# Filler matmuls made 32 columns wide, a scheduler model with tiling switches, and a lent PSUM bank, in an attention and linear-attention stack

## Chip, cores, metric

One core of one Trainium2 chip. The metric is the device time of one execution in microseconds (us). The experiments ran in three sessions on three chips, each with the kernel before in the same rounds; where sessions are compared, go by the ratio to it.

## The reference, cut to what matters

The input is one sequence of 2048 tokens, 512 wide. Four residual blocks run in turn: A, B, A, B.

```python
x = x + _A_ref(_layernorm(x), wq, wk, wv, wo)     # 32 query heads of 16, one shared key/value head
x = x + _B_ref(_layernorm(x), wqkv, wo)           # 32 heads of linear attention
# ... the same two once more
# A: p = softmax(q k^T / 4); o = p v        B: phi(q) (phi(k)^T v) / (phi(q) sum phi(k))
```

Block A needs 32 x 2048 x 2048 exponentials, twice. In tiles of 128 keys by 512 queries that is 2 x 2048 = 4096 tiles. Each needs a score matmul, an exponential and a value matmul, and the exponentials are the work that decides the time.

## The kernel before

The kernel is written as a list of operations with guessed durations. A small event-driven model of the chip runs at build time, decides the order of instructions on every engine, and the program is emitted in that fixed order. What the chip then does differently from the model changes the times, but not the order.

```python
LAT = {PE: 0.2, AC: 0.22, DV: 0.13, PO: 0.2, SP: 2.0}     # us until another engine sees a result
# ... inside fill(): one "set" of up to three score tiles in PSUM banks 3s, 3s+1, 3s+2
def f(e):
    return self.smm(e, got, 3 * s)              # three matmuls, 32 rows x 128 columns each
o  = add(PE, 0.2 + 0.014 * m, f, ...)                                  # score matmuls of a set
oe = add(AC, tac(m * 512), lambda e: e.activation(PTA[...], bank(3 * s, m * 512), ACTF.Exp, scale=SCALE), ...)
# ... add_pv(): a value matmul, 128 rows x 32 columns, into one of four column groups of bank 7
c = (j % NRG) * (4 // NRG) + j // NRG
return e.matmul(ps[32 * c:32 * c + 32, 7 * 512:8 * 512], lhsT=Vaug[:, kt, :], rhs=src, ...)
# ... dstep()/dpass(): the same work for a tile whose exponential VectorE computes, through bank 6,
#     as a polynomial in eight instructions a pair of tiles
```

A score tile thus goes one of two ways: ScalarE takes three at a time from banks 0 to 2 or 3 to 5, VectorE takes single tiles through bank 6. Projections and transposes ("misc") also go through bank 6, unless `SHARE` lets them use bank 5.

To hold TensorE's clock up, the model adds filler matmuls with zero weights whenever TensorE is idle and a running sum is low. That a TensorE with too little to do is granted less clock is what the kernel's author assumes here; what the runs show of it is the granted clock of 0.998 in the kernel before, against 0.851 when its 1234 fillers use 32 rows each (b_rows32, below).

```python
FILL, FILLW, FILLN = 0.6, 1.7, 512
SHARE = False

def idle(now):
    if not sc.order[PE] or streaming(now) > FILL * FILLW:
        return
    # ... (when bank 7 may be written)
    o = add(PE, 0.03 + FILLN * 0.41e-3, lambda e: e.matmul(bank(7, FILLN), lhsT=zer[:],
            rhs=maskx[:].bitcast(BF16)[:, 0:FILLN], start=not owned, stop=True, skip_group_check=True), ...)
```

The filler adds zeros to bank 7, where the value sums grow, and uses the whole array: 128 rows by 128 columns.

The softmax here doesn't subtract the row's maximum and nothing guards it: scores larger than these inputs give would overflow.

Of the kernel before, what the change touches and what calls it, by code (L numbers as in the profile page):

```python
# [5 lines left out]
BF16 = mybir.dt.bfloat16  # L6
# [9 lines left out]
STATS = {}  # L16
FLEX = 0.0


class Op:  # L20
    __slots__ = ("engs", "fn", "dur", "prio", "deps", "nleft", "succ", "rt", "guard", "acq", "uses", "rel", "cb",
                 "eng", "t0", "vis", "idx", "gidx", "waits", "marked", "val", "vc", "dma", "done", "name")

# [22 lines left out]
class Sched:  # L46


    def __init__(self, nc):
        self.nc = nc  # L50
        self.now = 0.0
        self.engs = [PE, AC, DV, PO, SP]
        self.tfree = {e: 0.0 for e in self.engs}
        self.pend = {e: [] for e in self.engs}
        self.ready = {e: [] for e in self.engs}
        self.order = {e: [] for e in self.engs}
        self.events = []
        self.seq = 0
        self.lastw = {}
        self.readers = {}  # L60
        self.all = []
        self.step = lambda now: False
        self.act_ok = lambda op: True
        self.idle = lambda now: None

    def add(self, engs, dur, fn, reads=(), writes=(), prio=5.0, guard=None, acq=(), uses=(), rel=(), cb=None, deps=(),
            dma=False, name=""):
        o = Op()
        o.engs = engs if isinstance(engs, tuple) else (engs,)
        o.dur = dur if isinstance(dur, dict) else {e: dur for e in o.engs}  # L70
        o.fn, o.prio, o.guard, o.acq, o.uses, o.rel, o.cb, o.dma, o.name = fn, prio, guard, acq, uses, rel, cb, dma, name
        o.rt, o.done, o.succ, o.marked = self.now, False, [], False
        ds = [d for d in deps if d is not None]
        for k in reads:
            w = self.lastw.get(k)
            if w is not None:
                ds.append(w)
        for k in writes:
            w = self.lastw.get(k)
            if w is not None:  # L80
                ds.append(w)
            ds += self.readers.get(k, ())
        for k in reads:
            self.readers.setdefault(k, []).append(o)
        for k in writes:
            self.lastw[k] = o
            self.readers[k] = []
        o.deps = []
        seen = set()
        for d in ds:  # L90
            if id(d) not in seen and d is not o:
                seen.add(id(d))
                o.deps.append(d)
        o.nleft = 0
        for d in o.deps:
            if d.done:
                o.rt = max(o.rt, self._vis(d, o))
            else:
                o.nleft += 1
                d.succ.append(o)  # L100
        if o.nleft == 0:
            self._queue(o)
        return o

    def _vis(self, d, o):
        if d.eng == PE and o.engs[0] == PE:
            return d.t0 + d.dur[PE]
        return d.vis

    def _queue(self, o):  # L110
        self.seq += 1
# [7 lines left out]
    def _try(self, e):  # L119
# [7 lines left out]
        if e == DV:  # L127
            cand = sorted(ready, key=lambda r: (r[0] + (FLEX if len(r[2].engs) > 1 and self.act_ok(r[2]) else 0.0), r[1]))
        for i, (p, s, o) in enumerate(cand):
            if o.done:  # L130
                continue
            if e == AC and len(o.engs) > 1 and not self.act_ok(o):
                continue
# [20 lines left out]
    def _start(self, e, o):  # L154
# [9 lines left out]
        for h in tuple(o.acq) + tuple(o.uses):  # L164
            for sl in h.pool.slots(h.idx, h.kind) if hasattr(h.pool, "slots") else (h.idx,):
                h.pool.hist[sl].append(o)
        end = self.now + o.dur[e]
        o.vis = end + (3.0 if o.dma else LAT[e])
        self.tfree[e] = end
        self.at(end, None)  # L170
        self.at(o.vis, None)
# [142 lines left out]
def bass_interleave_layers__grouped_kv_mqa__linear_attn_block__prompt_kernel(  # L314
# [20 lines left out]
    NRG, NM = P // RG, RG // DH  # L335
    FILL, FILLW, FILLN = 0.6, 1.7, 512
    SHARE = False
    FINE = (0, 3)
# [121 lines left out]
    def layer_norm(t, prio, cb, win=None):  # L460
# [15 lines left out]
        def tr(e):  # L476
# [3 lines left out]
            return i  # L480
        o = add(PE, 0.45, tr, reads=["ident"], deps=[o], uses=[hx], acq=[hb], rel=[hx], prio=prio, name="tr")

# [5 lines left out]
    def proj(h, mms, n, reads, prio, chunk=2, name="proj"):  # L488

        o = None  # L490
        for c in range(0, len(mms), chunk):
# [6 lines left out]
            kw = dict(acq=[h]) if c == 0 else dict(uses=[h], deps=[o])  # L498
            o = add(PE, len(part) * (0.03 + n * 0.36e-3), f, reads=reads, prio=prio, name=name, **kw)
        return o  # L500
# [18 lines left out]
    def v_proj(L, t0, n, prio):  # L519
        h = H_()  # L520

        def f(e):
# [4 lines left out]
            return k  # L527
        o = add(PE, 0.16 * n, f, reads=["wv"] + [("xnT", t) for t in range(t0, t0 + n)], acq=[h], prio=prio, name="vp")

# [18 lines left out]
    def q_tile(L, t, prio):  # L548
        h = H_()
        o = None  # L550
        for c in range(0, NG, 2):
# [6 lines left out]
            kw = dict(acq=[h]) if c == 0 else dict(uses=[h], deps=[o])  # L558
            o = add(PE, 0.55, f, reads=["wq", ("xnT", t)], prio=prio, name="qt", **kw)

# [8 lines left out]
    class Ctl:  # L569
# [75 lines left out]
        def add_pv(self, p, src, hold, dep, last):  # L645
# [9 lines left out]
            def cb(o):  # L655
# [10 lines left out]
                if sum(self.count[u]) == 64:  # L666
                    self.norm(u, o)

            def f(e):
                c = (j % NRG) * (4 // NRG) + j // NRG  # L670
                return e.matmul(ps[32 * c:32 * c + 32, 7 * 512:8 * 512], lhsT=Vaug[:, kt, :], rhs=src, start=opened[0], stop=opened[1],  # L671
                                skip_group_check=True)
            o = add(PE, 0.1, f, reads=[("V", kt)], deps=[dep], uses=[hold], rel=[hold] if last else [], prio=2.0 + 1e-4 * u, guard=guard, cb=cb, name="pv")
            return o

        def norm(self, u, last):
# [13 lines left out]
            def tr(e):  # L690
                for qs in range(4):
                    i = e.transpose(bank(ht.idx, P, qs * P), Eo[:, he.idx, qs * P:(qs + 1) * P], identf[:])
                return i
            o = add(PE, 1.0, tr, reads=["identf"], deps=[oe], acq=[ht, hos] if par == 0 else [ht], uses=[he], rel=[he], prio=1.2, name="trA")
            o = add(DV, 0.168, lambda e: e.reciprocal(rden[:, hr.idx, :].unsqueeze(2), bank(ht.idx).rearrange("p (a c) -> p a c", c=32)[:, :, DH:DH + 1]),
# [60 lines left out]
        def fill(self, s, got, kind):  # L756
# [9 lines left out]
            m = len(got)  # L766

            def f(e):
                return self.smm(e, got, 3 * s)
            o = add(PE, 0.2 + 0.014 * m if RG == 32 else 0.05 + 0.14 * m, f, reads=self.keys(got), deps=prev, uses=[h], prio=0.0, name="sA")  # L770
            hp = Holder(p_pta)
# [18 lines left out]
        def dstep(self):  # L790
# [36 lines left out]
            banks.hist[6] = []  # L827
            o = add(PE, 0.22, lambda e: self.smm(e, [p], 6), reads=self.keys([p]), deps=prev, uses=[h], prio=1.5, name="sD")
            o = add(DV, tdv(512), lambda e: e.tensor_scalar(out=xT[:, hx.idx, i * 512:(i + 1) * 512], in0=bank(6), scalar1=SCALE * LOG2E * 65536.0,  # L829
# [45 lines left out]

    def streaming(now):

        tot = 0.0
        for o in reversed(sc.order[PE]):
            if o.t0 + 1.5 < now - FILLW:  # L880
                break
            st = {"pv": 0.071, "sA": 0.2 if RG == 32 else 0.4, "dummy": 0.2}.get(o.name, 0.85 * o.dur[PE])
            end = o.t0 + o.dur[PE]
            if end > now - FILLW:
                tot += st * min(1.0, (end - (now - FILLW)) / o.dur[PE])
        return tot

    def idle(now):
        if not sc.order[PE] or streaming(now) > FILL * FILLW:
            return  # L890
        u = ctl.acc_owner
        owned = u >= 0 and 0 < sum(ctl.count[u]) < 64
        if not owned and not banks.free[7]:
            return
        if owned and now < sc.tfree[AC] < now + 0.1:
            return
        o = add(PE, 0.03 + FILLN * 0.41e-3, lambda e: e.matmul(bank(7, FILLN), lhsT=zer[:], rhs=maskx[:].bitcast(BF16)[:, 0:FILLN], start=not owned, stop=True, skip_group_check=True),  # L897
                reads=["mask", "zer"], deps=[] if owned else list(banks.hist[7]), prio=9.0, name="dummy")
        banks.hist[7].append(o)
        sc._try(PE)  # L900

# [5 lines left out]
    def epi_tr(L, qb, g, hos, fine):  # L907
# [4 lines left out]
        def tr(e):  # L912
# [3 lines left out]
            return i  # L916
        o = add(PE, 0.45, tr, reads=["ident", ("Osb", g % 2, 0), ("Osb", g % 2, 1)], acq=[h], uses=[hos], rel=[hos], writes=keys, prio=pr, name="otr")

# [57 lines left out]
    def pq_tile(t, pr):  # L976
# [3 lines left out]
        for g in range(NG):  # L980
# [4 lines left out]
            kw = dict(acq=[h]) if g == 0 else dict(uses=[h], deps=[o])  # L985
            o = add(PE, 0.27, f, reads=["wqkv", ("xnT", t)], prio=pr, name="pq", **kw)
        phi(h, o, pqT[:, :, ts], [("pq", g, t) for g in range(NG)], 2.4, tiled=True)

    def kv_block(L, b):
        tl = KVB[b]  # L990
        n, final = len(tl), b == len(KVB) - 1
        for hh in range(2):
            h = H_()
            o = None
            for i, t in enumerate(tl):
# [10 lines left out]
                rd = [t] if i > 0 else tl  # L1006
                o = add(PE, 0.22, f, reads=[(k, tt) for k in ("pk", "vB") for tt in rd], prio=3.4, name="kv", **kw)
            dst = kvacc if b == 0 else kvtmp
# [33 lines left out]
    def b_tile(L, t, nxt):  # L1042
# [4 lines left out]
        def den(e):  # L1047
            for g in range(NG):
                i = e.matmul(bank(hd.idx, P, g * P), lhsT=zb[:, g, :], rhs=pqT[:, g, ts], start=True, stop=True)
            return i  # L1050
        o = add(PE, 0.3, den, reads=[("zb", g) for g in range(NG)] + [("pq", g, t) for g in range(NG)], acq=[win, hd], prio=pr - 0.4, name="den")
        o = add(AC, tac(512), lambda e: e.activation(e_buf[:, he.idx, :], bank(hd.idx), ACTF.Ln, bias=1e-6), deps=[o], uses=[hd], acq=[he], rel=[hd], prio=0.4 + 0.01 * t, name="ln")
# [74 lines left out]
```

## Time and profile before

| | before |
|---|---|
| median time (3 runs) | 1779.86 us (1778.36 to 1780.38) |
| ScalarE (ACT) busy | 1728.1 us, 97% |
| VectorE (DVE) busy | 1554.0 us, 87% |
| tiles on ACT / on DVE | 3618 / 478 |
| fillers | 1234 |
| mean granted clock | 0.998 |

From the page of the kernel before: busy times by engine (PEld is TensorE loading weights), the granted TensorE clock in 40 slices (9 is 90% or more), the chain of waits, and groups of instructions (count, busy us, mean ns, idle us of the engine ahead of them and what ended it).

```profile
PE 1683.0 (95%) x11642; PEld 533.4 (30%) x11642; DVE 1554.0 (87%) x2767; ACT 1728.1 (97%) x1452; POOL 31.3 (2%) x46
...
PEclk9999999999999999999999999999999999999999
...
ACT 62%; PE 19%; DVE 17%; issue 1%; DMA 0%; POOL 0%; SPq 0%
...
L775 ACT ACTIVATE PTA<-ps_all 128x1536 bf16<-128x1536 f32 x1207 | 1644.0, 1569 | 7.7 <-PE ps_all L635 6.3
L635 PE MATMUL ps_all<-QT,Kr 32*128 32x512 bf16 x4096 | 611.3, 385 | 39.8 <-ACT PTA L775 14.8
L671 PE MATMUL ps_all<-PTA,Vaug 128*32 128x512 bf16 x3618 | 520.1, 390 | 8.2 <-DVE Eo L683 7.8
L897 PE MATMUL ps_all<-maskx,zer 128*128 128x512 bf16 x1234 | 401.0, 386 | 0.0
L829 DVE TENSOR_SCALAR xT<-ps_all 128x512 int32<-128x512 f32 x478 | 327.4, 685 | 80.8 <-PE ps_all L635 78.9
```

ACT is the bound: 97% busy, and the exponentials (L775) wait only 6.3 us for TensorE in the whole run. TensorE looks nearly as busy, but 401 us of its time are fillers (L897). DVE has time to spare, and 78.9 us of its idle time is spent waiting for its own score tile (L829 waits for L635).

The waits of the kernel before (us in total, times, longest):

```profile
DVE xT L829 <- PE ps_all L635: 78.9, 129, 1.3
DVE e_buf L940 <- ACT e_buf L939: 45.2, 29, 2.8
DVE v_tok L958 <- PE ps_all L496: 25.3, 19, 3.1
...
DVE x_sb L933 <- PE ps_all L496: 11.1, 12, 2.2
```

The timeline of TensorE alone, kernel before (start us, us, engine, line, form rows*columns, count):

```profile
60.02 0.40 PE L671 MATMUL ps_all<-PTA,Vaug 128*32 128x512 bf16 x3
60.35 0.39 PE L897 MATMUL ps_all<-maskx,zer 128*128 128x512 bf16 x1
60.67 0.39 PE L635 MATMUL ps_all<-QT,Kr 32*128 32x512 bf16 x1
```

Three value matmuls of different column groups start within nanoseconds of each other (0.40 us in all for three of 0.39; over the trace 3 ns apart in the median). The filler, in another tiling, starts 0.33 us later, and the next tiling again 0.32 us later. Over the whole trace a change of tiling is 315 to 323 ns start to start in the median, by the kind of change, and two fillers in a row 226 ns.

### The profile page before, as it was taken

What the parts mean: (1) busy time and instruction counts of PE and PEld (TensorE: products, weight loads), DVE (VectorE), ACT (ScalarE), POOL (GpSimd) and SP (SyncE); (2) the same over time, 40 slices, a digit from 0 to 9 for tenths busy, and PEclk for the clock granted to TensorE, in tenths of its full rate; (3) what the DMA queues carried; (4) which work ended last, traced back from release to release, by engine and by line L of the source; (5) the groups of instructions that cost most, each with busy time, mean ns of one, the idle gap of its engine ahead of it and who ended that gap; (6) DMA issues with size and microseconds to landing.
All of it is one profiled execution on the core that took longest, in us unless ns stands there. A gap on an engine that the chain in (4) does not pass through costs nothing.

```text
span 1777.9 us, 27691 instructions
## 1 busy us (share of the span) xinstructions
PE 1683.0 (95%) x11642; PEld 533.4 (30%) x11642; DVE 1554.0 (87%) x2767; ACT 1728.1 (97%) x1452; POOL 31.3 (2%) x46
## 2 busy tenths in 40 slices
PE   7999999999999999999899999999999999999998
PEld 4222222222232222233442222322222322222334
DVE  7999997999887998878789999879998879978775
ACT  7999999999999999999699999999999999999996
POOL 0000000000000000000000000000000000000000
PEclk9999999999999999999999999999999999999999
DMA  3000000000000000000000000000000000000001
GB/s 120 1 1 1 1 1 1 1 1 1 1 1 1 1 1 1 1 1 1 1 1 1 1 1 1 1 1 1 1 1 1 1 1 1 1 1 1 1 1 48
DMA packets 7724, 9.14 MB, mean 5 GB/s; under 512 B 1456, under 2 KB 7088, under 8 KB 7600
## 3 DMA queue, kind: packets, MB, share of 16 engines
q1 hardware_dynamic: 7600, 7.37, 1.3%
q8 instruction: 91, 1.49, 0.3%
q14 instruction: 33, 0.27, 0.1%
HBM read 5.28 MB, written 2.10 MB: 4 GB/s over the span
## 4 chain that ended last, share of the span: by engine, by line
ACT 62%; PE 19%; DVE 17%; issue 1%; DMA 0%; POOL 0%; SPq 0%
ACT PTA L775 60%; PE ps_all L635 6%; PE ps_all L671 5%; PE ps_all L897 3%; DVE xT L829 3%; DVE PTD L851 3%; PE ps_all L496 2%; ACT e_buf L939 1%; DVE xs L847 1%; DVE xu L846 1%; DVE xs L850 1%; DVE stats L461 1%; PE ps_all L1060 1%; DVE xs L848 1%; DVE xu L849 1%
## 5 line engine op out<-in xcount | busy, mean ns | idle before, releaser
L775 ACT ACTIVATE PTA<-ps_all 128x1536 bf16<-128x1536 f32 x1207 | 1644.0, 1569 | 7.7 <-PE ps_all L635 6.3
L635 PE MATMUL ps_all<-QT,Kr 32*128 32x512 bf16 x4096 | 611.3, 385 | 39.8 <-ACT PTA L775 14.8
L671 PE MATMUL ps_all<-PTA,Vaug 128*32 128x512 bf16 x3618 | 520.1, 390 | 8.2 <-DVE Eo L683 7.8
L897 PE MATMUL ps_all<-maskx,zer 128*128 128x512 bf16 x1234 | 401.0, 386 | 0.0
L829 DVE TENSOR_SCALAR xT<-ps_all 128x512 int32<-128x512 f32 x478 | 327.4, 685 | 80.8 <-PE ps_all L635 78.9
L635 PEld LDWEIGHTS ps_all<-QT,Kr 32*128 32x128 bf16 x4096 | 147.2, 91 | 486.3 <-ACT PTA L775 188.1
L851 DVE SCALAR_TENSOR_TENSOR PTD<-xT,xs 128x1024 uint16<-128x1024 int32 x239 | 290.3, 1215 | 1.8
L671 PEld LDWEIGHTS ps_all<-PTA,Vaug 128*32 128x32 bf16 x3618 | 126.2, 93 | 319.0 <-issue 299.9
L846 DVE TENSOR_SCALAR xu<-xT 128x1024 f16<-128x1024 uint16 x239 | 164.3, 687 | 3.7
L847 DVE TENSOR_TENSOR xs<-xu 128x1024 f16<-128x1024 f16 x239 | 163.5, 684 | 2.9
L850 DVE TENSOR_TENSOR xs<-xs,xu 128x1024 f16<-128x1024 f16 x239 | 163.0, 682 | 2.4
L897 PEld LDWEIGHTS ps_all<-maskx,zer 128*128 128x128 bf16 x1234 | 93.9, 97 | 196.5 <-issue 179.4
L671 PE MATMUL ps_all<-PTD,Vaug 128*32 128x512 bf16 x478 | 128.8, 388 | 18.2 <-DVE Eo L683 11.4
L848 DVE TENSOR_SCALAR xs<-xs 128x1024 f16<-128x1024 f16 x239 | 98.9, 414 | 1.7
L849 DVE TENSOR_SCALAR xu<-xu 128x1024 f16<-128x1024 f16 x239 | 99.2, 415 | 0.0
L496 PE MATMUL ps_all<-wqkv_sb,xnT 128*128 128x512 bf16 x256 | 68.7, 382 | 1.5 <-DVE xT L829 0.9
L940 DVE TENSOR_SCALAR e_buf<-e_buf 128x512 f32<-128x512 f32 x64 | 27.1, 423 | 45.4 <-ACT e_buf L939 45.2
L469 POOL TENSOR_TENSOR rstd<-veps,mhalf 128x1 f32<-128x1 f32 x30 | 27.8, 925 | 1668.5 <-DVE veps L467 1668.5
L939 ACT ACTIVATE e_buf<-ps_all 128x512 f32<-128x512 f32 x64 | 46.0, 719 | 4.8 <-PE ps_all L496 3.1
L671 PEld LDWEIGHTS ps_all<-PTD,Vaug 128*32 128x32 bf16 x478 | 28.2, 93 | 65.2 <-DVE PTD L851 30.7
L461 DVE BATCH_NORM_STATS2 stats<-x_sb 128x6 f32<-128x512 bf16 x64 | 43.2, 680 | 3.8 <-DMA x_sb<-in_A_x_dram 2.9
L683 DVE COPY Eo<-ps_all 128x512 f32<-128x512 f32 x62 | 42.4, 684 | 4.3 <-PE ps_all L671 3.7
(87 smaller groups left out, 825.9 us busy)
## 6 DMA issues: line engine op xcount, KB each, us to landing
out_dram<-x_sb SPq DMA_DIRECT2D x16, 128.0 KB, 1.7
x_sb<-in_A_x_dram SPq DMA_DIRECT2D x3, 512.0 KB, 6.9
wqkv_sb<-in_B_wqkv_dram SPq DMA_DIRECT2D x1, 1536.0 KB, 11.3
x_sb<-in_A_x_dram SPq DMA_DIRECT2D x2, 256.0 KB, 3.1
wq_sb<-in_A_wq_dram SPq DMA_DIRECT2D x1, 512.0 KB, 5.1
wo_sb<-in_A_wo_dram SPq DMA_DIRECT2D x1, 512.0 KB, 8.3
wo_sb<-in_B_wo_dram SPq DMA_DIRECT2D x1, 512.0 KB, 10.9
wk_sb<-in_A_wk_dram SPq DMA_DIRECT2D x1, 16.0 KB, 2.5
```

The lines of the kernel that those rows point to most:

```text
L496: i = e.matmul(bank(h.idx, n), lhsT=l, rhs=r, start=(c + k == 0), stop=(c + k == len(mms) - 1))
L635: x = e.matmul(bank(b0 + k), lhsT=Kr[r, m, kt * P:(kt + 1) * P], rhs=QT[r, self.units[u][0] % 2, gs, q0:q0 + n], start=True, stop=True)
L671: return e.matmul(ps[32 * c:32 * c + 32, 7 * 512:8 * 512], lhsT=Vaug[:, kt, :], rhs=src, start=opened[0], stop=opened[1], skip_group_check ...
L775: oe = add(AC, tac(m * 512), lambda e: e.activation(PTA[:, hp.idx, 0:m * 512], bank(3 * s, m * 512), ACTF.Exp, scale=SCALE), deps=[o] + pr ...
L829: o = add(DV, tdv(512), lambda e: e.tensor_scalar(out=xT[:, hx.idx, i * 512:(i + 1) * 512], in0=bank(6), scalar1=SCALE * LOG2E * 65536.0, ...
L846: o = add(DV, tdv(w, 0.52), lambda e: e.tensor_scalar(out=u_, in0=lo, scalar1=1.0 / 65536, scalar2=-0.5, op0=ALU.mult, op1=ALU.add), deps= ...
L847: o1 = add(DV, tdv(w, 0.52), lambda e: e.tensor_tensor(out=s_, in0=u_, in1=u_, op=ALU.mult), deps=[o] + c["prev"], name="xsq", **kw)
L848: o2 = add(DV, tdv(w, 0.26), lambda e: e.tensor_scalar(out=s_, in0=s_, scalar1=XK, scalar2=-XW, op0=ALU.mult, op1=ALU.add), deps=[o1], nam ...
L849: o3 = add(DV, tdv(w, 0.26), lambda e: e.tensor_scalar(out=u_, in0=u_, scalar1=1.0, scalar2=XL, op0=ALU.mult, op1=ALU.add), deps=[o1], nam ...
L850: o4 = add(DV, tdv(w, 0.52), lambda e: e.tensor_tensor(out=s_, in0=s_, in1=u_, op=ALU.mult), deps=[o2, o3], name="xc", **kw)
L851: o5 = add(DV, tdv(w), lambda e: e.scalar_tensor_tensor(out=PTD[:, hp.idx, 0:w].bitcast(U16), in0=xT[:, k, 0:w], scalar=2.0 ** -9, in1=s_, ...
L897: o = add(PE, 0.03 + FILLN * 0.41e-3, lambda e: e.matmul(bank(7, FILLN), lhsT=zer[:], rhs=maskx[:].bitcast(BF16)[:, 0:FILLN], start=not ow ...
```

## The change

The intent is to make fillers cheaper and to feed DVE better. Its parts:

1. After values or scores a filler takes the tiling of the value matmuls (32 columns), so that no tiling switch (322 ns start to start above, for 226) is needed between values and filler. When to place one is decided by modelled row activity.
2. The model now counts 0.1 us for a tiling switch (315 to 323 ns for 226 in the trace above) and 0.217 us for a pass, and it lets tiles of different groups overlap (3 ns apart above). It may also issue a set of score matmuls twice.
3. `SHARE = True`: misc operations may borrow bank 5. Then a set of ScalarE has two banks, and its exponential is 1024 wide, not 1536.

```diff
+SWITCH, PASS = 0.1, 0.217
...
+    def pe_need(self, o):
+        k, g = o.pk
+        if k != self.pk:
+            return self.pend_t + SWITCH
+        return self.pend_t if k == "F" else max([self.pgrp.get(x, 0.0) for x in g])
...
-    FILL, FILLW, FILLN = 0.6, 1.7, 512
-    SHARE = False
+    AWIN, ATGT, ATGT2 = 1.7, 0.5, 0.6
+    SHARE = True
...
             def f(e):
+                if twice:
+                    self.smm(e, got, 3 * s)
                 return self.smm(e, got, 3 * s)
-            o = add(PE, 0.2 + 0.014 * m ..., f, ...)
+            o = add(PE, PASS * (-(-m * RG // P)) * (2 if twice else 1), f, ...)
...
-        if not sc.order[PE] or streaming(now) > FILL * FILLW:
+        if activity(now) > ATGT:
             return
...
+        kind = "F" if sc.pk == "F" else "P"
+        need = sc.pend_t + (0.0 if sc.pk == kind else SWITCH)
...
+            c = min(range(4), key=lambda c: sc.pgrp.get(c, 0.0) if sc.pk == "P" else c)
+            f = lambda e: e.matmul(ps[32 * c:32 * c + 32, 7 * 512:8 * 512], lhsT=zer[:, 0:32],
+                                   rhs=maskx[:].bitcast(BF16)[:, 0:512], start=not owned, stop=True, ...)
+            pk = ("P", (c,))
```

(The diff is cut to its core; durations of projections and transposes were revised too.)

## The prediction

> **What bounds the kernel now.** The page shows ScalarE (ACT) busy 1728.1 of 1777.9 us (97%), VectorE (DVE) 1554.0 (87%), TensorE (PE) 1683.0 (95%). The chain of waits is 62% ACT, 60% of it the exponentials. In windows of 50 us ACT is at 49.2 to 50 nearly everywhere; it loses time only in the first 34 us, at the layer change (850 to 920) and in the last 75 us. PE's 95% is not real need: 401 us are zero-weight filler matmuls (1234). So the kernel is ACT-bound, and the span can only fall by (a) moving score tiles from ACT to DVE or (b) shortening ramp, layer change and tail. Of 4096 tiles ACT takes 3618, at 1331 ns start to start for three (0.444 us a tile); DVE takes 478, at about 2.41 us each (the start-to-start times in the timeline: 2x601 + 3x602 + 2x335 + 1135 ns a pair).
>
> **What the change does.**
> 1. Fillers 128 columns wide become 32 wide, in the tiling of the value matmuls. In the timeline a change of tiling costs 315 to 322 ns start to start, against 220 to 226 ns within one tiling, so about 0.1 us each. [...] 624 value-to-filler changes disappear: about 62 us of PE time, off ACT's path (ACT waits for score matmuls only 6.3 us in all). The gain is only that DVE's own score tile arrives earlier.
> 2. The scheduler's model gets real PE durations, so DVE's fixed order should fit better. ACT's and DVE's durations do not change.
> 3. Lending bank 5 lets projections avoid bank 6, which feeds DVE. It makes some exponentials 1024 wide, about 50 ns extra per extra instruction: a few us of ACT.
> 4. Doubled score matmuls fill PE time only.
>
> **Worth.** DVE is idle 224 us. By the waits: 78.9 us for its score tile (129 waits), 45.2 for ACT's exponential in the linear block (unchanged in kind), 25.3 and 11.1 for projections. I expect 40 to 90 us of this to go, that is 15 to 35 more tiles on DVE, each taking 0.444 us from ACT: 7 to 15 us. Ramp, layer change and tail: 0 to 8 us. Minus 2 to 5 us for narrower exponentials. A ceiling, an estimate from the same numbers: were DVE idle only 40 us, 64 tiles more, 28 us, 1.6%. So over 2% is nearly out of reach.
>
> **Clock.** The trace shows two windows of 3.413 us at half clock[...]. I expect 0 to 8 such windows after; around the one near 1063 us ACT lost 1.8 us in its 50 us slice, so this costs under 8 us.
>
> **Predicted: 1764 us, 1746 to 1783 (8 in 10). Faster by over 2%: 0.05; within 2%: 0.90; slower by over 2%: 0.05.**
>
> **What would show it.** ACT still about 97% busy and top of the chain. DVE's tiles 490 to 515, its busy time up 20 to 60 us, its wait for score tiles under 55 us. A few hundred 1024-wide exponentials, with more ACT instructions. Fillers 128x32, no value-to-filler change near 320 ns. Clock mean at least 0.99.
>
> **What would make it wrong.** Row activity judged too low by the chip: many half-clock windows, PE then late for ACT and ACT waits well over 20 us (slower). Doubled score matmuls delaying ACT's next set. Two-bank sets leaving PE too little lead, ACT idling between 905 ns exponentials. On the other side, a shorter layer change and tail by more than 15 us.

## The result, and the profile after

The kernel after takes 1860.8 us (1854.31 to 1864.32, 4 runs) against 1780.12 us for the kernel before in the same comparison. The ratio is 1.0444, with a 95% interval of 1.0409 to 1.048: slower by 4.4%. Ratios here are the mean time of one kernel's runs over that of the other's of the same rounds, so not quite the ratio of the medians quoted.

The page of the kernel after:

```profile
PE 1694.5 (91%) x11488; PEld 487.2 (26%) x11488; DVE 1623.1 (87%) x2924; ACT 1731.6 (93%) x1543; POOL 28.7 (2%) x46
...
PEclk9998897676998999985999886997799968678999
...
ACT 61%; PE 30%; DVE 8%; DMA 0%; issue 0%; SPq 0%; POOL 0%
...
L809 ACT ACTIVATE PTA<-ps_all 128x1536 bf16<-128x1536 f32 (+1 forms) x1297 | 1645.6, 1444 | 81.9 <-PE ps_all L661 77.3
...
L863 DVE TENSOR_SCALAR xT<-ps_all 128x512 int32<-128x512 f32 x516 | 355.7, 689 | 90.4 <-PE ps_all L661 88.0
...
L947 PE MATMUL ps_all<-maskx,zer 128*32 128x512 bf16 x845 | 294.4, 449 | 0.0
```

The clock row is what to look at first. The mean granted clock fell from 0.998 to 0.873: the clock record has 474 us at half clock in 25 stretches, up to 51.2 us long, where the kernel before has two of 3.4 us. The exponentials now wait 77.3 us for score matmuls (L809 waits for L661), where they waited 6.3. The work did move as planned: DVE has 516 tiles (478 before), and ACT has 3580.

Two 50 us windows of the kernel after (start:end, length, busy us of PE, PEld, DVE, ACT, POOL with counts, then the clock, DMA share, GB/s):

```profile
250.00:300.00 50.00, 46.70 (x338) 14.85 (x338) 40.44 (x73) 50.00 (x49) 0.55 (x1) 1.00 0.00 1
300.00:350.00 50.00, 48.41 (x255) 9.74 (x252) 41.90 (x71) 43.60 (x33) 0.00 (x0) 0.57 0.00 1
```

At full clock ACT has no idle time at all in this stretch. At a clock of 0.57 TensorE is busier and does fewer matmuls (255 for 338), and ACT loses 6.4 us in 50. (PE's busy time includes more than the streaming of columns: a score matmul counts 385 ns in the kernel before, while fillers of the same 512 columns in one group start 216 ns apart. So it doesn't show how active the array is.)

The timeline of the kernel after, around a group of values:

```profile
59.86 0.40 PE L698 MATMUL ps_all<-PTA,Vaug 128*32 128x512 bf16 x3
59.87 0.60 PE L947 MATMUL ps_all<-maskx,zer 128*32 128x512 bf16 x2
...
60.88 0.10 PEld L661 LDWEIGHTS ps_all<-QT,Kr 32*128 32x128 bf16 x4 [0.91 <-ACT PTA L809]
```

This is the key. The first filler starts 0.01 us after the first value matmul, not after the values. Values occupy three of the four column groups, the filler goes to the fourth, and all four start within about 0.01 us of each other. Of 432 fillers that directly follow a value matmul, 417 start under 0.1 us after it. So do 118 of the 283 that follow another filler.

To see what that does, I counted row activity from the trace. Each matmul was taken to stream for its columns at the granted clock, 222 ns for 512 columns at the full clock and twice that at half. Both figures are assumptions. The trace of this kernel shows narrow fillers that do not run side by side 216 to 217 ns apart, start to start, in 109 of 125 cases at the full clock, and 391 ns in the median at half (38 pairs), so both are long. Where this matters, the figure for an assumed 213 ns, which is a little short, stands beside it. At any moment the share of the 128 rows in use was noted, matmuls side by side in the same rows counting once. Taking the fillers out of that count shows what they add:

| kernel | fillers in the trace | row time they add | per filler |
|---|---|---|---|
| before | 1234 | 273.7 us | 222 ns |
| after | 937 | 89.3 us | 95 ns |

(With 213 ns a pass: 213 and 94 ns per filler.)

Then I cut the time into windows of 3.413 us, in step with the clock record (in the kernel after, each of the 25 stretches at half clock is a whole multiple of that, from 1 to 15). There, 23 of the 25 windows just ahead of a drop of the clock had rows in use for under 0.40 of the time; of the 378 windows after which the full clock went on, 6 did (24 and 26 with 213 ns). TensorE was never idle for long in the windows ahead of a drop: by the same count no idle gap was over 0.81 us in 24 of them, and the longest was 1.7 us in one, at the layer change.

### The profile page after: what moved, and what is told of

It is laid out like the page before. It is cut to its first block, busy times and chain, and to the rows that moved or that the text cites. A ratio compares the mean times of both kernels' runs of the same rounds, so it can differ in the third digit from the quotient of the medians.

```text
span 1862.2 us, 27675 instructions
## 1 busy us (share of the span) xinstructions
PE 1694.5 (91%) x11488; PEld 487.2 (26%) x11488; DVE 1623.1 (87%) x2924; ACT 1731.6 (93%) x1543; POOL 28.7 (2%) x46
## 4 chain that ended last, share of the span: by engine, by line
ACT 61%; PE 30%; DVE 8%; DMA 0%; issue 0%; SPq 0%; POOL 0%
ACT PTA L809 59%; PE ps_all L661 12%; PE ps_all L698 10%; PE ps_all L947 2%; PE ps_all L522 2%; ACT e_buf L991 2%; PE ps_all L719 1%; DVE xT L863 1%; PE ps_all L1112 1%; DVE PTD L885 1%; DVE stats L487 1%; DVE xs L881 1%; DVE xs L884 0%; DVE xu L880 0%; DVE xn_buf L498 0%; DVE Kr L537 0%
## 5 line engine op out<-in xcount | busy, mean ns | idle before, releaser
L809 ACT ACTIVATE PTA<-ps_all 128x1536 bf16<-128x1536 f32 (+1 forms) x1297 | 1645.6, 1444 | 81.9 <-PE ps_all L661 77.3
L661 PE MATMUL ps_all<-QT,Kr 32*128 32x512 bf16 x4239 | 739.7, 436 | 106.9 <-ACT PTA L809 86.5
L698 PE MATMUL ps_all<-PTA,Vaug 128*32 128x512 bf16 x3580 | 620.9, 440 | 24.6 <-ACT PTA L809 21.2
L661 PEld LDWEIGHTS ps_all<-QT,Kr 32*128 32x128 bf16 x4239 | 162.3, 93 | 653.9 <-ACT PTA L809 379.6
L885 DVE SCALAR_TENSOR_TENSOR PTD<-xT,xs 128x1024 uint16<-128x1024 int32 (+1 forms) x259 | 314.3, 1215 | 0.8
L947 PE MATMUL ps_all<-maskx,zer 128*32 128x512 bf16 x845 | 294.4, 449 | 0.0
L880 DVE TENSOR_SCALAR xu<-xT 128x1024 f16<-128x1024 uint16 (+1 forms) x259 | 177.3, 685 | 1.2
L881 DVE TENSOR_TENSOR xs<-xu 128x1024 f16<-128x1024 f16 (+1 forms) x259 | 177.0, 684 | 0.9
L884 DVE TENSOR_TENSOR xs<-xs,xu 128x1024 f16<-128x1024 f16 (+1 forms) x259 | 176.9, 685 | 1.0
L882 DVE TENSOR_SCALAR xs<-xs 128x1024 f16<-128x1024 f16 (+1 forms) x259 | 108.8, 420 | 0.9
L883 DVE TENSOR_SCALAR xu<-xu 128x1024 f16<-128x1024 f16 (+1 forms) x259 | 109.1, 421 | 0.0
```

Source lines behind the costliest of these rows:

```text
L661: x = e.matmul(bank(b0 + k), lhsT=Kr[r, m, kt * P:(kt + 1) * P], rhs=QT[r, self.units[u][0] % 2, gs, q0:q0 + n], start=True, stop=True)
L809: oe = add(AC, tac(m * 512), lambda e: e.activation(PTA[:, hp.idx, 0:m * 512], bank(3 * s, m * 512), ACTF.Exp, scale=SCALE), deps=[o] + pr ...
L880: o = add(DV, tdv(w, 0.52), lambda e: e.tensor_scalar(out=u_, in0=lo, scalar1=1.0 / 65536, scalar2=-0.5, op0=ALU.mult, op1=ALU.add), deps= ...
L881: o1 = add(DV, tdv(w, 0.52), lambda e: e.tensor_tensor(out=s_, in0=u_, in1=u_, op=ALU.mult), deps=[o] + c["prev"], name="xsq", **kw)
L882: o2 = add(DV, tdv(w, 0.26), lambda e: e.tensor_scalar(out=s_, in0=s_, scalar1=XK, scalar2=-XW, op0=ALU.mult, op1=ALU.add), deps=[o1], nam ...
L883: o3 = add(DV, tdv(w, 0.26), lambda e: e.tensor_scalar(out=u_, in0=u_, scalar1=1.0, scalar2=XL, op0=ALU.mult, op1=ALU.add), deps=[o1], nam ...
```

## The experiments

The theories at the outset:

- **A**: fillers in a free column group run beside the values and add no time of row activity.
- **B**: a filler of 32 columns counts less because it uses a quarter of the cells.
- **C**: the new order has too few fillers (937 for 1234), wherever they run.

All twelve runs gave correct results. "Half clock" is from the clock record of the profiled run, "per filler" is the row time as above.

| run | median us | before, same rounds | ratio | clock | half clock us | per filler ns | DVE tiles |
|---|---|---|---|---|---|---|---|
| after | 1860.8 | 1780.12 | 1.0444 | 0.873 | 474 | 95 | 516 |
| a_same | 1769.87 | 1784.23 | 0.9925 | 0.994 | 20 | 212 | 516 |
| a_wide | 1771.34 | 1784.23 | 0.9934 | 0.999 | 4 | 222 | 516 |
| b_narrow_same | 1776.28 | 1784.23 | 0.9962 | 0.995 | 17 | 218 | 478 |
| b_narrow_next | 1826.34 | 1784.23 | 1.0237 | 0.934 | 244 | 91 | 478 |
| b_rows32 | 1937.08 | 1778.71 | 1.0874 | 0.851 | 578 | | 478 |
| a_atgt65 | 1789.38 | 1778.71 | 1.0061 | 0.977 | 82 | 72 | 494 |
| a_same_noshare | 1775.87 | 1778.71 | 0.9981 | 0.998 | 7 | 213 | 465 |
| b_share | 1797.47 | 1778.71 | 1.0121 | 0.999 | 3 | 222 | 542 |
| b_share_same | 1787.25 | 1779.09 | 1.0052 | 0.992 | 27 | 217 | 542 |
| a_same_once | 1770.23 | 1779.09 | 0.9944 | 0.996 | 14 | 208 | 517 |
| a_same_atgt55 | 1764.08 | 1779.09 | 0.9916 | 1.000 | 0 | 212 | 516 |
| a_max55 | 1762.87 | 1779.09 | 0.9911 | 1.000 | 0 | 209 | 522 |

### a_same: the filler in the group just used

```diff
 c = min(range(4), key=lambda c: ...)
+last = sc.order[PE][-1]
+cc = real.get(id(last), last.pk[1][0]) if last.pk[0] == "P" else c
-f = lambda e: e.matmul(ps[32 * c:32 * c + 32, 7 * 512:8 * 512], ...)
+f = lambda e: e.matmul(ps[32 * cc:32 * cc + 32, 7 * 512:8 * 512], ...)
```

The model still books group `c`, so the order of instructions is the same on every engine; this was compared. Only where the 845 narrow fillers land differs.

> The kernel after with the same order of instructions on every engine; a narrow filler goes into the column group that the instruction ahead of it used, where before it went into the group free longest. Theory A (a filler in a free group runs beside the value matmuls and adds no time of row activity; in the kernel after it added 95 ns a filler, the wide one 222): each filler adds about 200 ns, clock mean 0.97 or more, under 10 half-clock windows, 1745 to 1785 us. Theory B (a narrow filler counts less because it has a quarter of the columns): clock stays 0.85 to 0.90, 1845 to 1870 us. Theory C (the new order has too few fillers, 937 for 1234, wherever they are put): clock 0.88 to 0.94, above 1810 us.

Measured: 1769.87 us, clock 0.994, 212 ns a filler. The page, waits and timeline of this kernel:

```profile
PE 1632.3 (92%) x11488; PEld 509.7 (29%) x11488; DVE 1613.3 (91%) x2924; ACT 1713.8 (97%) x1543; POOL 29.1 (2%) x46
...
PEclk9999999999999999999999998999999999999999
```

```profile
DVE xT L863 <- PE ps_all L661: 29.2, 48, 1.6
...
ACT PTA L809 <- PE ps_all L661: 7.8, 14, 1.5
```

```profile
59.95 0.40 PE L698 MATMUL ps_all<-PTA,Vaug 128*32 128x512 bf16 x3
...
60.19 0.59 PE L951 MATMUL ps_all<-maskx,zer 128*32 128x512 bf16 x2
...
60.98 0.40 PE L661 MATMUL ps_all<-QT,Kr 32*128 32x512 bf16 x4 [0.19 <-ACT PTA L809]
```

The same fillers of the same width, 0.24 us after the values and not 0.01: the clock comes back, ACT's wait falls from 77.3 to 7.8 us, DVE's from 88.0 to 29.2. Theories B and C fall. The whole slow-down, and more, was in the choice of column group. Of the 93.5 us between the two profiled spans (1862.2 less 1768.7), 69.5 are ACT's wait for its score tiles.

### a_wide: every filler 128 columns again, in the order of the kernel after

```diff
-f = lambda e: e.matmul(ps[32 * c:32 * c + 32, 7 * 512:8 * 512], lhsT=zer[:, 0:32], ...)
+f = lambda e: e.matmul(bank(7), lhsT=zer[:], ...)
```

> The kernel after, same order, with every filler 128 columns wide again. Theories A and B both: clock 0.97 or more; tiling switches come back (about 0.1 us each for some 700 fillers, TensorE only), 1750 to 1790 us. Theory C: clock 0.88 to 0.94, above 1810 us.

Measured: 1771.34 us, clock 0.999. A filler that fills all columns adds the 222 ns of a whole pass again and not 95 (in the timeline of the kernel before one starts 0.33 us after the values, not beside them), and 937 of them are enough for this clock. This also refutes C. With a_same at 1769.87, narrow and wide fillers cost about the same once both are serial: in this order the switches cost nothing that shows in the time.

### b_narrow_same and b_narrow_next: the same test in the kernel before

All 1234 fillers become 32 wide in the unchanged order of the kernel before. They go into the column group of the value or filler just ahead (`_same`), or into the next group (`_next`); a filler after anything else goes into group 0 in both.

```diff
+grp[id(o_)] = (grp[id(before)] + STEP) % 4 if id(before) in grp else 0      # STEP 0: same, 1: next
-lambda e: e.matmul(bank(7, FILLN), lhsT=zer[:], ...)
+e.matmul(ps[32 * c:32 * c + 32, 7 * 512:8 * 512], lhsT=zer[:, 0:32], ...)   # c = grp[id(o)]
```

> The kernel before, same order, its 1234 fillers made 32 columns wide, in the column group of the value matmul or filler just ahead. Theory A: a filler still adds about 200 ns of row activity, clock 0.98 or more, 1765 to 1785 us. Theory B: a quarter of the columns, clock under 0.93, above 1820 us.

> As the run before, but each filler in the next column group, not that of the instruction ahead of it. Theory A: fillers after values and after fillers run beside them, under 130 ns of row activity a filler, clock 0.80 to 0.93, above 1830 us. Theory B: the same as the run before, within 1%.

Measured: 1776.28 us at clock 0.995, and 1826.34 us at 0.934 (a little under the bounds that I gave for A, 1830 us and 0.93, so the time misses the forecast by 4 us and the clock lies at its edge). 531 of the 630 fillers that follow values start alongside them in the second, 10 of 625 in the first. The clock rows of the two pages, the first kernel's and then the second's:

```profile
PEclk9999999999999999999999999999999999999999
```

```profile
PEclk9899999989999869989999799998999995998999
```

Nothing of the change but the filler is in these kernels, and the column group alone makes 2.8% (1826.34 over 1776.28). And the intended saving is there: the switch between value and filler is gone (226 ns start to start in the median, 322 before), and the kernel is 0.4% faster than before (interval 0.9946 to 0.9978). By what path is not shown: the waits for score matmuls hardly moved (ACT's 6.4 us for 6.3, DVE's 77.0 for 78.9).

### b_rows32: a quarter of the rows, all columns

```diff
-e.matmul(bank(7, FILLN), lhsT=zer[:], rhs=maskx[:].bitcast(BF16)[:, 0:FILLN], ...)
+e.matmul(bank(7, FILLN), lhsT=zer[0:RG, :], rhs=maskx[:].bitcast(BF16)[0:RG, 0:FILLN], ...)      # RG = 32
```

> The kernel before, same order, its fillers 128 columns wide but on 32 rows instead of 128 (a quarter of the cells, as in the narrow fillers, and serial). If the clock follows the share of rows in use: each filler counts a quarter, clock under 0.90, above 1830 us. If it follows the time in which any matmul streams: clock 0.98 or more, 1770 to 1790 us. If it follows cells: like the narrow fillers in the same group, which kept 0.995, so 0.98 or more.

Measured: 1937.08 us, clock 0.851. This filler has as many cells as the narrow one, and the narrow one kept the clock. The page of this kernel:

```profile
PE 1813.5 (94%) x11541; PEld 535.0 (28%) x11642; DVE 1562.1 (81%) x2767; ACT 1748.4 (90%) x1452; POOL 31.3 (2%) x46
...
PEclk8778769776989859999797889777699989989998
```

TensorE counts as busy for 94% of the span, and the granted clock is 0.851 all the same. One thing is not clean here: 326 of these fillers start alongside a score matmul that follows and 105 alongside one ahead of them (other rows, same tiling), so they lose some streaming time too. The windows help to tell the measures apart. In the 32 windows ahead of a drop in this kernel something streamed for a median 0.60 of the time, which is well above such windows in the kernel after (0.49); the share of rows in use was 0.37 and 0.38. An estimate from the windows of four traces (before, after, b_narrow_next, b_rows32): the best single cut by row activity puts about 25 of their 1771 windows at full clock on the wrong side, the best cut by streaming time about 75, by cells in use about 80. So of these three measures the change's own, row activity, fits these windows best.

### a_atgt65: more fillers, still in the free group

```diff
-AWIN, ATGT, ATGT2 = 1.7, 0.5, 0.6
+AWIN, ATGT, ATGT2 = 1.7, 0.65, 0.75
```

> The kernel after as it is (fillers in the group free longest), with the activity targets raised from 0.5 and 0.6 to 0.65 and 0.75: 1516 fillers for 937. Theory A (they run alongside): still 100 to 130 ns of row activity a filler, more in all, so clock 0.90 to 0.97 and 1785 to 1835 us, short of the corrected kernel. Theory C (only too few fillers): clock 0.98 or more and under 1785 us.

Measured: 1789.38 us, clock 0.977. The time is in the range forecast for A, the clock a little above it, and a filler adds even less, 72 ns. 1485 fillers in the trace add 106 us of row time, where the 937 of a_same add 199. A higher target hides the fault in part. It also leaves DVE 494 tiles, so this run is not a clean measure of the clock alone.

### a_same_noshare and b_share: what the lent bank is worth

```diff
-SHARE = True          # a_same_noshare, from a_same
+SHARE = False
```

```diff
-SHARE = False         # b_share, from the kernel before
+SHARE = True
```

> The corrected kernel after (fillers in the column group just used), bank 5 not lent: its schedule gives DVE 465 tiles for 516, and two 1024-wide exponentials for 311. If the lent bank is what moves work to DVE: 51 tiles at 0.444 us, less 52 ns for each of the 102 extra exponentials, so about 17 us slower than the corrected kernel, 1780 to 1792 us, no faster than before. If the scheduler's new durations are what helps: 1765 to 1775 us. Clock 0.98 or more in both.

> The kernel before with only the bank lent (old durations, wide fillers): DVE gets 542 tiles for 478. If the lent bank is the gain: 64 tiles at 0.444 us less some 120 extra exponentials at 52 ns, 22 us less, 1755 to 1768 us, clock 0.98 or more. If the old durations leave TensorE too late for two-bank sets: ACT waits for TensorE over 20 us and the time is 1775 us or more.

Measured: without lending, 1775.87 us (0.9981 of before), 4 us better than the range that I gave. The rest of the change (new durations, new rule for placing fillers, narrow fillers run one after another) is thus worth about 0.2% (interval 0.9968 to 0.9993), and lending on top of it brings it to about 0.75%. The new durations were not tried alone. Lending alone, in the old order, gave 1797.47 us: slower by 1.2% at a clock of 0.999, where I expected 22 us less if lending was the gain; the other forecast, TensorE too late for ACT, is the one that came true. The chain and a wait of that kernel:

```profile
PE 41%; ACT 32%; DVE 25%; issue 2%; DMA 0%; SPq 0%; ACTq 0%
```

```profile
DVE xT L829 <- PE ps_all L635: 34.9, 69, 1.3
ACT PTA L775 <- PE ps_all L635: 25.8, 79, 0.8
```

DVE is fed better (34.9 us of wait, 78.9 before) and takes 542 tiles. But TensorE now heads the chain, and ACT waits 25.8 us for it. The same bank is a gain in one order and a loss in the other.

### b_share_same: is it the fillers' switches?

The two edits b_share and b_narrow_same together.

> The kernel before with the bank lent, same order as that run (1797 us, clock 0.999), its fillers narrow and in the column group just used. If lending the bank was slow because the fillers' tiling switches (552 after values, 0.1 us each) made TensorE late: ACT's waits for TensorE fall from 25.8 us to under 15 us and the time is 1760 to 1780 us. If the order made with the old TensorE durations is the cause: 1785 to 1797 us, no more than the 0.4% that the same edit gave the kernel before.

Measured: 1787.25 us, clock 0.992, in between: ACT's wait for TensorE stays at 25.4 us, and the kernel is still 0.5% slower than before. Narrow fillers without the switch win back a part (0.7% of time, against 0.4% in the kernel before). That the order made with the old durations is the rest is argued, not shown: the kernels that lend the bank at a gain also place fillers by another rule, and no run changed the durations alone.

### a_same_once: no score matmul twice

`twice = False` in a_same: 4096 score matmuls for 4239.

> The corrected kernel after with no score matmul issued twice: 4096 for 4239, and 942 fillers. If doubling matters for the clock: more windows under 0.40 of row activity, clock 0.95 to 0.99, 1775 to 1800 us. If not: 1764 to 1776 us, clock 0.99.

Measured: 1770.23 us, clock 0.996. It is within the range for "not": the doubled matmuls make no difference clear of noise at this target (ratio 0.9944, a_same 0.9925).

### a_same_atgt55 and a_max55: a version better than both

The first is a_same with targets 0.55 and 0.65. The second corrects the model as well, so that it books the group that the filler uses:

```diff
-AWIN, ATGT, ATGT2 = 1.7, 0.5, 0.6
+AWIN, ATGT, ATGT2 = 1.7, 0.55, 0.65
-c = min(range(4), key=lambda c: sc.pgrp.get(c, 0.0) if sc.pk == "P" else c)
+c = max(range(4), key=lambda c: sc.pgrp.get(c, 0.0) if sc.pk == "P" else -c)
```

> Candidate: the corrected kernel after with targets 0.55 and 0.65: 1046 fillers, 516 tiles on DVE. Clock 0.99 or more, 1760 to 1772 us, with a smaller spread than the corrected kernel's 10.8 us.

> Candidate: the kernel after with the filler in the group used last, in the scheduler's model too, targets 0.55 and 0.65: 1134 fillers, 522 tiles on DVE. Clock 0.99 or more, 1758 to 1772 us; faster than before by 0.5 to 1.3%.

Measured: 1764.08 and 1762.87 us, both without a half-clock window in the profiled run. The page of a_max55:

```profile
PE 1642.0 (93%) x11617; PEld 519.3 (30%) x11702; DVE 1626.1 (92%) x2940; ACT 1710.7 (97%) x1548; POOL 27.4 (2%) x46
...
L809 ACT ACTIVATE PTA<-ps_all 128x1536 bf16<-128x1536 f32 (+1 forms) x1300 | 1625.2, 1513 | 4.5 <-PE ps_all L661 3.3
```

It beats the kernel before by 0.9% (ratio 0.9911, interval 0.9896 to 0.9925), with a spread of 2 us. ACT is the bound again and waits 3.3 us for TensorE.

## Why the prediction was wrong

- **What bounds the kernel** (ACT; only moved tiles or a shorter ramp could help): right for the kernel before, and again for the corrected kernels.
- **Tiles moved**: 490 to 515 forecast, 516 measured. "A few hundred 1024-wide exponentials": 311. DVE's wait for score tiles was to be under 55 us: 88.0 in the kernel after, 29.2 in a_same, once the fillers are put right.
- **The switch between value and filler**: about 0.1 us each, and little gain. Right: b_narrow_same gains 0.4%.
- **"I expect 0 to 8 such windows after ... so this costs under 8 us": this is the step that failed.** There were 139 such windows, in 25 stretches, 474 us, and they cost about 91 us (1860.8 less 1769.87). I took a narrow filler to add the same row activity as a wide one, without saying so. It added 95 ns and not 222, because it ran beside the values. I wrote that the filler would sit "in the tiling of the value matmuls" and drew only one consequence of it, the saved switch. The other is that matmuls of that tiling in different column groups start side by side: the trace before showed values 3 ns apart. That was in front of me, and the diff's `min` chooses the group in which it happens.
- **Size of the miss**: with the group alone corrected, the same order takes 1769.87 us, within the range of 1746 to 1783 and 6 us above the 1764 that I gave. The failed step was the whole miss.
- **The lent bank**: I expected it to win tiles and cost a few us of ACT. That holds only together with the rest of the change; alone it costs 1.2%. I hadn't seen the interaction.
- **What would make it wrong**: my first item named half-clock windows and ACT waits over 20 us, but I gave "slower by over 2%" a chance of 0.05, without asking how many nanoseconds of row activity one filler adds.

The kernel's author had a model that allowed for this: `activity` counts overlapping values once, and `idle` waits until all in flight has ended. But the model's times are not kept on the chip, only its order is. On the chip nothing made the filler wait for the values ahead of it: 417 of 432 started within 0.1 us of them. The group "free longest" is one in which nothing holds the filler back; in the group just used it is held (in a_same 9 of 437 start within 0.1 us).

How a drop grew to 19 us in the mean (474 over 25): of the windows at half clock in the kernel after that were followed by another, the median had rows in use for 0.69 of the time; of those followed by the full clock, 0.80. (Counted with the 391 ns that the trace shows for a pass at half clock, both are about 0.07 to 0.08 lower.) Ahead of a drop the median was 0.38. So windows filled well above those ahead of a drop still did not bring the clock back, for up to 51.2 us on end. And at half clock TensorE gets less done: passes start 391 ns apart for 216 to 217, and the 50 us at a clock of 0.57 hold 255 matmuls for 338. That this is why a drop lasts was not tested by an experiment.

## What to carry to other kernels

An instruction that is there for its duration must be held by something on the chip, here the same column group (9 of 437 fillers started within 0.1 us of the values in a_same, 417 of 432 in the kernel after); a start time in a scheduler's model doesn't hold it. When a padding operation changes shape, ask what it can now run beside, and measure what one of them adds before counting how many there are. Look at the granted clock first: one row of the profile told this case.
